# v loaded in rows of four tokens and put in place by TensorE, with score products of a quarter of the keys each

## The chip, the cores and the metric

The kernel runs on one core of one Trainium2 chip. The metric is the device time of one launch in microseconds. A profiled execution gives the span from the first to the last instruction and a trace of every instruction and every DMA packet. The engines are PE (TensorE matmul; PEld its weight loads), DVE (VectorE), ACT (ScalarE), POOL (GpSimd) and SP (SyncE, which issues most DMAs here).

## What is computed

There are 8 batches, 8 heads, 576 tokens and 64 values per head. First a sliding-window attention with a linear bias per head, then a mixing of the 64 lowest frequencies along the sequence by complex 512x512 weights, one pair of matrices for each frequency, and a last product with a ReLU. q, k, v, the weights and the output are float32.

```python
scores = scale * np.matmul(q, k.transpose(0, 1, 3, 2))
rel = pos[:, None] - pos[None, :]
mask = (rel >= 0) & (rel < 128)
scores = np.where(mask, scores + bias[None], -1000000000.0)   # bias = -slope(h) * |rel|
attn = softmax(scores)
x = matmul(attn, v), heads side by side                       # (8, 576, 512)
X = np.fft.rfft(x, axis=1)                                    # first 64 modes
Yr = Xr @ w_r - Xi @ w_i ;  Yi = Xr @ w_i + Xi @ w_r          # per mode
u = x + irfft(Y)
out = u + relu(u @ w_ch)
```

## The kernel before

**Units and slots.** The attention is cut into 32 units. A unit is a pair of heads s and a batch b. The first 8 units are head pair 0 for all batches (group 0); the other 24 go batch by batch through head pairs 1, 2, 3 (group 1). A loop runs one slot per unit, and the instructions are placed by hand: `manual_schedule` keeps every engine's order as the program writes it. Slot n works on several units at once: the scores of unit n, the transposes of q and k of unit n+1, the casts of n+2, the product of the weights with v (av) of unit n-1, and the spectrum of unit n-2.

**What one unit needs.** q and k come by one DMA each (`_load_unit`, L356), 9 tokens in a row of 2304 bytes. POOL casts them to bf16 (L391). `_tr` turns them by 18 transposes each on PE (L414) into a PSUM buffer `tqk`, and `_evac` copies that to SBUF on ACT (L422). `_score` makes the scores in two halves w = 0, 1 into one PSUM tile `sc`, of two banks (L441; the last 64 keys at L449); ACT takes the exponential (L453), DVE multiplies with a mask that holds bias and window (L458, L463). `_av` multiplies with v and a column of ones (L487, L493) and DVE divides (L498 to L504). `_spectrum` (L533) turns x into modes: in group 0 after each unit, 5 matmuls, in group 1 after every third, 15 matmuls.

**The keys' order.** In a block of 128 keys the key's token number is spread over the partitions: partition 64 r + p holds token 2 p + r. The two score matmuls of a block and head therefore read every second key, and the rows of `sc` come out in that order; the mask's distance has a step of -2 per partition, and 127 is added in the upper half. v has the same order, since two tokens in sequence are one row of 512 bytes in DRAM. `_load_v` (L367) issues two DMAs per unit, one per head, and `_cast_v` (L403) moves and casts it on POOL with four instructions into one of three buffers `vb`, from which av reads. The last 64 tokens (`vt`) come on their own.

**The weights.** A ring of 48 KB in each partition takes the weights in the order of use: 64 parts of 0.5 MB for group 0 (rows of the first head pair), then 64 parts of 1.5 MB for group 1. `_load_w` (L652) issues a part as soon as its space in the ring has been used, from inside `_modes`, whose matmuls are L692 (`acc`). The products of group 0 are spread over the slots from number 10 on (arguments w0 and w1 of `_slot`); `_select` (L572 to L579) prepares their operand every few slots, in a PSUM tile that the spectrum also uses. The products of group 1 follow after the last slot, with other work between them (the product with w_ch, L746, and from the modes that are ready already the first of the inverse transforms, `_z_early`, L779 and L783). A last part, `_finish`, ends the inverse transform and writes the output.

**Order on the queues.** All loads but `vt` go through SP's one queue. Before the slots it gets the loads of 16 units and the first weight parts; in each later slot one more unit, the v of the unit three before it, and the weight parts that have become free. There are nine buffers for q and for k (`QK`) and six for v (`VB`).

In a slot PE's order is: score w = 0, transposes of q, transposes of k, weight products w0, score w = 1, spectrum, av, weight products w1:

```python
    if n < N:
        _score(g, n, 0)
    if n + 1 < N:
        _tr(g, n + 1, 0)
        _evac(g, n + 1, 0)
        _tr(g, n + 1, 1)
```

Of the kernel before, what the change touches and what calls it, by code (L numbers as in the profile page):

```python
# [9 lines left out]
FP32 = mybir.dt.float32  # L10
# [32 lines left out]
def kernel(  # L43
# [50 lines left out]
    with tc.manual_schedule(engines={ET.SP, ET.PE, ET.Activation, ET.DVE, ET.Pool}):  # L94
        with ExitStack() as wctx:
# [5 lines left out]
            with ExitStack() as actx:  # L101
# [3 lines left out]
                if JOINT[0] != 2:  # L105
# [8 lines left out]
                g.ps2 = actx.enter_context(  # L114
                    tc.tile_pool(name="ps2", bufs=1, space=bass.MemoryType.PSUM))
                g.ps1 = actx.enter_context(
                    tc.tile_pool(name="ps1", bufs=2, space=bass.MemoryType.PSUM))
                g.pss = actx.enter_context(
                    tc.tile_pool(name="pss", bufs=1, space=bass.MemoryType.PSUM))

# [10 lines left out]
                with tc.tile_pool(name="tmpc", bufs=1, side="right") as tp:  # L131
                    _consts(g, tp)
                    _cast_qk(g, 0)
                    for s in GROUPS[0]:
                        _load_vt(g, s)
                    _cast_qk(g, 1)
                    _cast_v(g, 0)
                    for s in GROUPS[0]:
                        _cast_vt(g, s)
                    _tr(g, 0, 0)  # L140
                    _tr(g, 0, 1)
                    _evac(g, 0, 0)
                    _evac(g, 0, 1)
                    first = dict.fromkeys(u[1] for u in units[:2])
                    rest = [s for s in range(NP) if s not in first]
                    for s in first:
                        _mask(g, tp, s)
                    for n in range(3):
                        _slot(g, n, [], [])
                    for s in rest:  # L150
                        _mask(g, tp, s)
# [85 lines left out]
def _consts(g, tp):  # L237
# [4 lines left out]
    mi = tp.tile([P, 2, NM], I32)  # L242
    nc.gpsimd.iota(mi, [[0, 2], [1, NM]], base=0, channel_multiplier=0)
    reli = tp.tile([P, 256], I32)
    nc.gpsimd.iota(reli, [[1, 256]], base=0, channel_multiplier=-2)
    rel3i = tp.tile([P, 64], I32)
    nc.gpsimd.iota(rel3i, [[1, 64]], base=0, channel_multiplier=-1)
    make_identity(nc, g.ident_b)
# [37 lines left out]
    rel = tp.tile([P, 512], FP32)  # L286
    g.rel = rel
    nc.vector.tensor_copy(rel[:, 0:256], reli)
    nc.vector.tensor_scalar_add(rel[64:128, 0:256], rel[64:128, 0:256], 127.0)
    nc.vector.tensor_copy(rel[:, 448:512], rel3i)  # L290
    nc.vector.tensor_scalar_add(rel[64:128, 448:512], rel[64:128, 448:512], 64.0)
    off = tp.tile([P, 256], FP32)
# [68 lines left out]
def _load_v(g, n):  # L361

    _, s, b = g.units[n]
    u = g.unit.setdefault(n, Ctx())
    u.v = g.vpool.tile([P, 2, 2, 2, g.D], FP32, tag="v", name=f"v{n}")
    for hh in range(2):
        g.nc.sync.dma_start(  # L367
            out=u.v[:, hh].rearrange("p k r d -> p k (r d)"),
            in_=g.v[b, 2 * s + hh, 0:512, :].rearrange("(k p r) d -> p k (r d)", k=2, r=2))


def _load_vt(g, s):
# [22 lines left out]
def _cast_v(g, n):  # L395

    u = g.unit[n]
    u.vb = g.vbs[n % 3]
    o = u.vb[:, :, 0 : g.D].rearrange("p (k i h) d -> p i k h d", k=2, i=2)
    v = u.v.rearrange("p h k r d -> p r k h d")  # L400
    for r in range(2):
        for i in range(2):
            g.nc.gpsimd.tensor_copy(  # L403
                o[64 * r : 64 * r + 64, i], v[64 * i : 64 * i + 64, r])


def _tr(g, n, w):
# [11 lines left out]
def _evac(g, n, w):  # L419
    u = g.unit[n]  # L420
    dst = g.work.tile([P, g.S], BF16, tag=f"qkT{w}", name=f"qkT{w}")
    g.nc.scalar.copy(  # L422
        dst.rearrange("c (p r) -> c p r", r=g.R), u.tp[w].rearrange("c r p -> c p r"))
    u.qk = getattr(u, "qk", []) + [dst]


def _score(g, n, w):


    nc = g.nc  # L430
    u = g.unit[n]
    s = g.units[n][1]
    qT, kT = u.qk
    sc = g.pss.tile([P, 2, 512], FP32, tag="sc", name="sc")
    for i in range(2):
        c = 2 * w + i
        nq = 256 if c < 3 else 192
        for r in range(2):
            for hh in range(2):
                hs = slice(64 * hh, 64 * hh + 64)  # L440
                nc.tensor.matmul(  # L441
                    sc[64 * r : 64 * r + 64, hh, 256 * i : 256 * i + nq],
                    lhsT=kT[hs, c * P + r : c * P + P : 2], rhs=qT[hs, c * P : c * P + nq],
                    start=True, stop=True, tile_position=(64 * hh, 64 * r))
    if w:
        for r in range(2):
            for hh in range(2):
                hs = slice(64 * hh, 64 * hh + 64)
                nc.tensor.matmul(  # L449
                    sc[64 * r : 64 * r + 64, hh, 448:512], lhsT=kT[hs, 512:576],  # L450
                    rhs=qT[hs, 512:576], start=True, stop=True, tile_position=(64 * hh, 64 * r))
    a = g.work.tile([P, 2, 512], BF16, tag=f"att{w}", name=f"att{w}")
    nc.scalar.activation(a, sc, AF.Exp, scale=1.0 / math.sqrt(g.D))  # L453
    u.att = getattr(u, "att", []) + [a]
    if not w:
        a = a.rearrange("p h (i q) -> p h i q", i=2)
        m = g.mask[:, s, :, 0:256].unsqueeze(2).broadcast_to([P, 2, 2, 256])
        nc.vector.tensor_tensor(out=a, in0=a, in1=m, op=ALU.mult)  # L458
# [124 lines left out]
def _slot(g, n, w0, w1):  # L583
# [7 lines left out]
    if n + 1 < N:  # L591
        _tr(g, n + 1, 0)
        _evac(g, n + 1, 0)
        _tr(g, n + 1, 1)
    if n == N + 1:
        _spectrum(g, n - 2)
    for w in w0:
# [1 line left out]
    if n < N:  # L599
        _score(g, n, 1)  # L600
    if n + 1 < N:
        _evac(g, n + 1, 1)
    if n + 2 < N:
        _cast_qk(g, n + 2)
    if n + 1 < N:
        _cast_v(g, n + 1)
    for j, grp in enumerate(GROUPS[1:]):
        for i, s in enumerate(grp):
            if n == g.first[j + 1] - 4 + i:
# [324 lines left out]
```

## Time and profile before

| | |
|---|---|
| median of 3 runs | 455.17 us (453.47 to 456.06) |
| the profiled execution's own time | 454.71 us |
| its span, first to last instruction | 452.9 us |
| mean granted clock of TensorE | 0.787 |
| attention: first exponential, last av | 11.8 us, about 165 us |
| weight products of group 1 | from about 169 to 413 us |
| the end (`_finish`) | 413 to 453 us |
| DMA in all | 173.85 MB, 51273 packets, mean 384 GB/s |
| of it v without its last 64 tokens | 64 DMAs of 128 KB, 16384 packets of 512 bytes |
| POOL in the casts of v (L403) | 128 of 498 ns mean, 63.7 us |

Busy times are shares of one engine's time; several engines are busy at once. In a group of instructions "idle before" is how long the engine stood still ahead of them, and after the arrow what ended it. The DMA share is the sum of the packets' times over 16 engines and the stretch, so it can be somewhat above 1 where packets overlap. The clock is the share of TensorE's full clock that was granted.

### The profile page before, as it was taken

The numbers are of one execution on the slowest core, as the hardware profiler recorded it, in microseconds if no ns is written. First come the engines' busy times: TensorE is split into PE (matmuls) and PEld (weight loads), VectorE is DVE, ScalarE is ACT, GpSimd is POOL, SyncE is SP. The second block draws the span as 40 slices with busy tenths as digits, with TensorE's granted clock in tenths as the row PEclk, the third lists the DMA queues.
The fourth block names the chain that finished last, engine by engine and source line by source line (L and its number), as shares of the span: only waits on it lengthen the run. The fifth ranks groups of instructions, "written<-read, shape, count | busy, mean of one in ns | idle before, by whom it ended". The sixth has DMA issues, their size and how long they took to land.

```text
span 452.9 us, 12955 instructions
## 1 busy us (share of the span) xinstructions
PE 303.4 (67%) x5543; PEld 205.8 (45%) x5543; DVE 221.0 (49%) x434; ACT 191.4 (42%) x302; POOL 151.5 (33%) x262
## 2 busy tenths in 40 slices
PE   2677788887888873225555656657555657777994
PEld 2565576666676762213333333333333334554562
DVE  8467757647575561012433443435434334552784
ACT  4887677656665821001222332223222122332773
POOL 7799789866785502020000000000000000002574
PEclk9988859856797975556888886888667568998999
DMA  8999999999999999999999999999999999991778
GB/s 253 353 348 310 387 314 379 377 388 371 390 364 399 415 416 433 422 432 428 431 426 429 428 430 424 430 429 431 425 430 428 431 425 430 429 419 63 271 266 299
DMA packets 51273, 173.85 MB, mean 384 GB/s; under 512 B 4880, under 2 KB 21264, under 8 KB 43024
## 3 DMA queue, kind: packets, MB, share of 16 engines
q1 hardware_dynamic: 50832, 171.99, 96.1%
q0 software_dynamic: 384, 1.05, 0.9%
q8 instruction: 43, 0.70, 0.6%
q14 instruction: 14, 0.11, 0.1%
HBM read 163.58 MB, written 9.44 MB: 382 GB/s over the span
## 4 chain that ended last, share of the span: by engine, by line
DMA 46%; PE 27%; ACT 11%; DVE 9%; issue 4%; POOL 2%; POOLq 0%; ACTq 0%; DVEq 0%
DMA ring<-in_moe_w_r_dram 37%; DMA ring<-in_moe_w_i_dram 9%; ACT att L453 6%; PE acc L692 4%; PE sc L441 4%; PE xt L533 3%; PE av L487 3%; ACT qkT L422 3%; PE tqk L414 2%; PE mm L830 2%; PE y L830 1%; PE mm L733 1%; PE xw L746 1%; DVE att L463 1%; DVE x_sb L501 1%
## 5 line engine op out<-in xcount | busy, mean ns | idle before, releaser
L692 PE MATMUL acc<-Xz,ring 128*128 128x32 bf16 x2048 | 69.7, 183 | 95.9 <-DMA ring<-in_moe_w_i_dram 48.3
L692 PEld LDWEIGHTS <-ring 128*128 128x128 bf16 x2048 | 60.4, 101 | 126.8 <-DMA ring<-in_moe_w_i_dram 61.5
L751 ACT CAST hl<-xw 64x512 bf16<-64x512 f32 x72 | 41.8, 581 | 125.3 <-PE xw L746 93.2
L752 DVE TENSOR_TENSOR hl<-xw,hl 64x512 bf16<-64x512 f32 x72 | 49.6, 689 | 63.5 <-ACT hl L751 63.1
L453 ACT ACTIVATE att<-sc 128x1024 bf16<-128x1024 f32 x64 | 65.6, 1025 | 31.5 <-PE sc L441 25.2
L403 POOL CAST vb<-v 64x256 bf16<-64x256 f32 x128 | 63.7, 498 | 22.4 <-PE av L487 15.3
L772 POOL MEMSET ZTa<- 32x512 bf16 x1 | 0.5, 515 | 189.4 <-ACT ZTa L769 189.4
L746 PE MATMUL xw<-wch,xT 128*128 128x512 bf16 x144 | 52.4, 502 | 0.2 <-ACT FT L346 0.2
L441 PE MATMUL sc<-qkT,qkT 64*64 64x256 bf16 (+1 forms) x512 | 32.6, 330 | 25.8 <-ACT qkT L422 15.3
L422 ACT COPY qkT<-tqk 128x576 bf16<-128x576 bf16 x64 | 40.7, 637 | 0.6 <-PE tqk L414 0.5
L414 PE MATMUL tqk<-ident_b,qkb 64*64 64x64 bf16 x1152 | 31.8, 215 | 8.4 <-POOL qkb L391 8.3
L414 PEld LDWEIGHTS <-qkb 64*64 64x64 bf16 x1152 | 31.3, 131 | 11.1 <-POOL qkb L391 10.4
L458 DVE TENSOR_TENSOR att<-att,mask 128x1024 bf16<-128x1024 bf16 x32 | 27.5, 858 | 13.2 <-ACT att L453 13.1
L487 PE MATMUL av<-vb,att 128*128 128x65 bf16 (+1 forms) x512 | 31.2, 216 | 1.5 <-DVE att L463 0.8
L579 ACT ACTIVATE Xz<-xz 128x192 bf16<-128x192 f32 (+1 forms) x24 | 7.5, 313 | 54.3 <-DVE Xz L578 54.0
L726 DVE COPY xT<-tp 128x512 bf16<-128x512 bf16 x36 | 15.2, 422 | 30.3 <-PE tp L724 30.0
L391 POOL CAST qkb<-q 128x576 bf16<-128x576 f32 x32 | 26.4, 825 | 5.4 <-PE tqk L414 1.8
L487 PEld LDWEIGHTS <-att 128*128 128x128 bf16 (+1 forms) x512 | 24.6, 112 | 7.0 <-DVE att L463 1.2
L441 PEld LDWEIGHTS <-qkT 64*64 64x64 bf16 x512 | 13.2, 120 | 30.7 <-ACT qkT L422 17.7
L391 POOL CAST qkb<-k 128x576 bf16<-128x576 f32 x32 | 26.1, 817 | 0.1
L463 DVE TENSOR_TENSOR att<-att,mask 128x1024 bf16<-128x1024 bf16 x32 | 25.1, 785 | 1.5 <-ACT att L453 1.1
L746 PEld LDWEIGHTS <-xT 128*128 128x128 bf16 x144 | 17.1, 125 | 18.3 <-issue 14.0
(108 smaller groups left out, 424.0 us busy)
## 6 DMA issues: line engine op xcount, KB each, us to landing
ring<-in_moe_w_r_dram SPq DMA_DIRECT2D x32, 1536.0 KB, 13.8
ring<-in_moe_w_i_dram SPq DMA_DIRECT2D x32, 1536.0 KB, 13.8
ring<-in_moe_w_r_dram SPq DMA_DIRECT2D x32, 512.0 KB, 6.8
ring<-in_moe_w_i_dram SPq DMA_DIRECT2D x32, 512.0 KB, 7.2
q<-in_q_dram SPq DMA_DIRECT2D x32, 288.0 KB, 6.7
k<-in_k_dram SPq DMA_DIRECT2D x32, 288.0 KB, 6.3
v<-in_v_dram SPq DMA_DIRECT2D x64, 128.0 KB, 5.7
out_dram<-o SPq DMA_DIRECT2D x32, 256.0 KB, 2.7
```

What stands on the lines that cost most here:

```text
L391: g.nc.gpsimd.tensor_copy(tb, t)
L403: g.nc.gpsimd.tensor_copy(o[64 * r : 64 * r + 64, i], v[64 * i : 64 * i + 64, r])
L414: g.nc.tensor.transpose(tp[hs, r, :], u.b[w][hs, r], g.ident_b[hs, hs], tile_position=(64 * hh, 64 * hh))
L422: g.nc.scalar.copy(dst.rearrange("c (p r) -> c p r", r=g.R), u.tp[w].rearrange("c r p -> c p r"))
L441: nc.tensor.matmul(sc[64 * r : 64 * r + 64, hh, 256 * i : 256 * i + nq], lhsT=kT[hs, c * P + r : c * P + P : 2], rhs=qT[hs, c * P : c * P ...
L453: nc.scalar.activation(a, sc, AF.Exp, scale=1.0 / math.sqrt(g.D))
L463: g.nc.vector.tensor_tensor(out=a, in0=a, in1=g.mask[:, g.units[n][1]], op=ALU.mult)
L487: nc.tensor.matmul(av[o, hh, col(t)], lhsT=att[c // 2][:, hh, q0 : q0 + m], rhs=u.vb[:, 2 * c + hh, 0 : D + 1], start=(j == 0), stop=(t < ...
L692: nc.tensor.matmul(acc[:, et, :, m0 - c0 : m0 - c0 + n, :], lhsT=wt[:, a, et * P : (et + 1) * P], rhs=X[:, a, 1 - w : 3 - w, m0 % MB : m0 ...
L746: nc.tensor.matmul(xw, lhsT=xT[:, dt], rhs=g.wch[:, dt], start=(dt == 0 and g.way[n] != "q"), stop=(dt == 3))
L751: nc.scalar.copy(g.hl[own, n, h], xw[own])
L752: nc.vector.tensor_tensor(out=g.hl[other, n, h], in0=xw[own], in1=g.hl[own, n, h], op=ALU.subtract)
```

## The change

v comes in rows of four tokens: 1024 bytes, one DMA per unit instead of two. In a block of 128 keys partition 32 r + p now holds token 4 p + r, so a score matmul takes a quarter of a block's keys, and there are twice as many of them, each on 64 rows and 32 columns of the array. The mask's distances follow. A row of v lies in the wrong partitions, so POOL only casts it, in one instruction, to a new tile `vc` (one unit earlier than before), and a new function `_place_v` puts it in place: 16 matmuls whose stationary side is 32 columns of the identity, each into a group of 32 columns, into a PSUM tile `vp`; then one copy to `vb`, on ACT for odd units and on DVE for even ones. To make room in PSUM there is one `tqk` buffer where there were two, and the transposes of k move behind the second score, with `_place_v` after them.

```diff
-                    tc.tile_pool(name="ps1", bufs=2, space=bass.MemoryType.PSUM))
+                    tc.tile_pool(name="ps1", bufs=1, space=bass.MemoryType.PSUM))
...
+                    _cast_v(g, 1)
                     for s in GROUPS[0]:
                         _cast_vt(g, s)
-                    _tr(g, 0, 0)
-                    _tr(g, 0, 1)
-                    _evac(g, 0, 0)
-                    _evac(g, 0, 1)
+                    for w in range(2):
+                        _tr(g, 0, w)
+                        _evac(g, 0, w)
+                    _place_v(g, 0)
...
-    nc.gpsimd.iota(reli, [[1, 256]], base=0, channel_multiplier=-2)
+    nc.gpsimd.iota(reli, [[1, 256]], base=0, channel_multiplier=-4)
...
-    nc.vector.tensor_scalar_add(rel[64:128, 0:256], rel[64:128, 0:256], 127.0)
+    for r in range(1, 4):
+        rs = slice(32 * r, 32 * r + 32)
+        nc.vector.tensor_scalar_add(rel[rs, 0:256], rel[rs, 0:256], 127.0 * r)
...
-    u.v = g.vpool.tile([P, 2, 2, 2, g.D], FP32, tag="v", name=f"v{n}")
-    for hh in range(2):
-        g.nc.sync.dma_start(
-            out=u.v[:, hh].rearrange("p k r d -> p k (r d)"),
-            in_=g.v[b, 2 * s + hh, 0:512, :].rearrange("(k p r) d -> p k (r d)", k=2, r=2))
+    u.v = g.vpool.tile([P, 2, 4, g.D], FP32, tag="v", name=f"v{n}")
+    g.nc.sync.dma_start(
+        out=u.v.rearrange("p h r d -> p h (r d)"),
+        in_=g.v[b, 2 * s : 2 * s + 2, 0:512, :].rearrange("h (p r) d -> p h (r d)", r=4))
...
 def _cast_v(g, n):
     u = g.unit[n]
+    u.vc = g.work.tile([P, 4, 2, g.D], BF16, tag="vc", name="vc")
+    g.nc.gpsimd.tensor_copy(u.vc, u.v.rearrange("p h r d -> p r h d"))
+
+
+def _place_v(g, n):
+    nc = g.nc
+    u = g.unit[n]
     u.vb = g.vbs[n % 3]
-    o = u.vb[:, :, 0 : g.D].rearrange("p (k i h) d -> p i k h d", k=2, i=2)
-    v = u.v.rearrange("p h k r d -> p r k h d")
-    for r in range(2):
-        for i in range(2):
-            g.nc.gpsimd.tensor_copy(
-                o[64 * r : 64 * r + 64, i], v[64 * i : 64 * i + 64, r])
+    ps = g.ps1.tile([P, 4, 2, g.D], FP32, tag="vp", name="vp")
+    for c in range(4):
+        cs = slice(32 * c, 32 * c + 32)
+        for r in range(4):
+            nc.tensor.matmul(
+                ps[32 * r : 32 * r + 32, c].rearrange("p h d -> p (h d)"),
+                lhsT=g.ident_b[:, cs], rhs=u.vc[:, r].rearrange("p h d -> p (h d)"),
+                start=True, stop=True, tile_position=(0, 32 * r))
+    o = u.vb[:, :, 0 : g.D].rearrange("p (c h) d -> p c h d", c=4)
+    if n % 2:
+        nc.scalar.copy(o, ps)
+    else:
+        nc.vector.tensor_copy(o, ps)
...
-        for r in range(2):
+        for r in range(4):
             for hh in range(2):
                 hs = slice(64 * hh, 64 * hh + 64)
                 nc.tensor.matmul(
-                    sc[64 * r : 64 * r + 64, hh, 256 * i : 256 * i + nq],
-                    lhsT=kT[hs, c * P + r : c * P + P : 2], rhs=qT[hs, c * P : c * P + nq],
-                    start=True, stop=True, tile_position=(64 * hh, 64 * r))
+                    sc[32 * r : 32 * r + 32, hh, 256 * i : 256 * i + nq],
+                    lhsT=kT[hs, c * P + r : c * P + P : 4], rhs=qT[hs, c * P : c * P + nq],
+                    start=True, stop=True, tile_position=(64 * hh, 32 * r))
...
         _tr(g, n + 1, 0)
         _evac(g, n + 1, 0)
-        _tr(g, n + 1, 1)
...
     if n < N:
         _score(g, n, 1)
     if n + 1 < N:
+        _tr(g, n + 1, 1)
         _evac(g, n + 1, 1)
+        _place_v(g, n + 1)
     if n + 2 < N:
         _cast_qk(g, n + 2)
-    if n + 1 < N:
-        _cast_v(g, n + 1)
+        _cast_v(g, n + 2)
```

## The prediction

> **What bounds the kernel now.** I read the page first, then busy times by stretch, then SP's waits, then the chain around the end of the attention, and last PE's timeline of single slots.
>
> ```profile
> span 452.9 us, 12955 instructions
> ...
> DMA  8999999999999999999999999999999999991778
> GB/s 253 353 348 310 387 314 379 377 388 371 390 364 399 415 416 433 422 432 428 431 426 429 428 430 424 430 429 431 425 430 428 431 425 430 429 419 63 271 266 299
> ...
> DMA 46%; PE 27%; ACT 11%; DVE 9%; issue 4%; POOL 2%; POOLq 0%; ACTq 0%; DVEq 0%
> ```
>
> The DMA row is at 9 from the second slice to the 36th, about 412 us: the queue never runs dry. Only the rate changes, 310 to 399 GB/s while q, k and v are mixed in, about 430 once only weights flow.
>
> ```profile
> 12.00:57.00 45.00, 33.29 (x748) 25.74 (x747) 30.02 (x64) 34.18 (x46) 39.65 (x66) 0.89 1.05 351
> 57.00:166.00 109.00, 90.47 (x2165) 73.60 (x2165) 69.88 (x150) 71.81 (x101) 75.77 (x129) 0.79 1.03 380
> 166.00:412.00 246.00, 143.14 (x2210) 84.47 (x2210) 86.26 (x153) 55.36 (x106) 5.27 (x21) 0.73 1.00 423
> ```
>
> Columns: stretch, its length, busy PE, PEld, DVE, ACT, POOL, granted clock, DMA share, GB/s. The attention (12 to 165) has a DMA share of 1.03 to 1.05 and engines that are 60 to 90% busy: two things run side by side, a full DMA queue and a compute chain that lives on what was loaded ahead. SP's waits from 60 to 166 tell which is ahead:
>
> ```profile
> SPq L356 <- DMA ring<-in_moe_w_i_dram: 8.7, 10, 0.9
> SPq L652 <- PE acc L692: 5.6, 11, 1.5
> SPq L367 <- DMA q<-in_q_dram: 5.3, 10, 1.7
> ```
>
> SP waits more for earlier landings than for PE to free the ring. The first ring space was free when its products ended at 58.2 us; SP issued into it at 67.08. So compute is ahead of the issue, and DMA sets the pace; the lead is used up only at the end:
>
> ```profile
> 164.90 0.36 PE acc L692 x10
> 165.26 11.07 DMA ring<-in_moe_w_r_dram
> ...
> 177.24 13.74 DMA ring<-in_moe_w_r_dram
> ```
>
> At 165.26 SP issues a 1.5 MB part the moment PE frees its space, and it lands 11.07 us later. Its own transfer takes 3.66 us at 430 GB/s, and the quickest q load (288 KB, 0.69 us of transfer) took 3.1 us to land, so 2.4 us are overhead. The rest, **5.0 us**, it stood behind other transfers. This is the margin: compute may end the attention later by 5.0 us less what DMA gains before DMA runs dry. After 166 everything hangs on the 64 large weight parts in sequence and a tail of 41 us that the change does not touch. With g the DMA time saved and s the slip of the attention's end:
>
> change = -g + max(0, s + g - 5.0).
>
> If s is over 5 - g, it is s - 5, whatever g is.
>
> **The DMA part, g.** By the packet records of the trace, 16384 packets of 512 B took 28.5 ns each, 29.2 us on each of 16 engines; 8192 of 2304 B took 103.0, 8192 of 12288 B 461. After it there are 8192 of 1024 B: on the line between 512 and 2304 that is 49.8 ns, 25.5 us; 32 DMAs fewer save 512 completion packets of 9.5 ns, 0.3 us. g = 29.2 - 25.5 + 0.3 = **4.0 us**. Bounds: 0, if a 1024 B packet costs two of 512; 9.5, if it moves at the 12288 B rate (38.4 ns, 19.7 us). I take 4, the nearest rows. [...]
>
> **POOL.** Four casts of 64x256 (498 ns) become one of 128x512: the rows of 128x512 are 617 and 714 ns. That frees about 1.3 us of POOL per unit. It counts only where PE waits for POOL's q and k casts (slots 6 to 9, of 4.67, 4.25, 5.19 and 5.52 us between the first exponentials of L453). With POOL gone PE or ACT sets them at about 4.3 to 4.6, the last with a selection: **-1.2 us**. The cast also no longer waits for av (15.3 us of POOL idle), and DVE's mask products, 858 and 785 ns against 690 when POOL rests, may shorten: **-0.7**, between 0 and -3.
>
> **PE, the place matmuls.** The nearest row is 16 matmuls of 128x32 by 128, zp:
>
> ```profile
> 392.70 1.03 PE L746 MATMUL xw<-wch,xT 128*128 128x512 bf16 x4
> 393.66 0.47 PE L783 MATMUL zp<-ident_b,ZT 128*32 128x128 bf16 x16
> 393.95 1.05 PE L779 MATMUL zwp<-wch,ZT 128*32 128x512 bf16 x16
> ```
>
> zp holds PE from 393.66 to 393.95, 0.29 us at full clock; at half, by four steps of 0.106 as in zlp at 414.9, 0.43. The step from the last xw (393.35) to zp is 0.31 where xw follow each other by 0.215: a change of tile shape costs 0.095 (0.12 at half clock, from the transposes to acc at 94.2). After the change the order is score 64x32, transposes 64x64, weight products 128x128, score 64x32, last keys and transposes 64x64, place 128x32, av 128x128: three to four such changes more per unit, 0.3 to 0.4 us.
>
> **PE, the scores.** Twice the matmuls, 64x32. Four of 64x64 now start within 10 ns and the next four 0.13 to 0.20 us later, so four column groups side by side cost nothing more; zp's four at once speak for it. If eight don't run at once, it costs up to 0.25 us per score, 16 us in all. I take 0.
>
> **PE, the moved transposes.** With one tqk buffer the k transposes wait for ACT's copy of q and stand behind the second score. Behind them on PE wait place, spectrum, av and the next score. What that costs depends on the slot:
>
> ```profile
> 76.28 0.39 PE L441 MATMUL sc<-qkT,qkT 64*64 64x256 bf16 x8
> 76.47 0.23 PE L449 MATMUL sc<-qkT,qkT 64*64 64x64 bf16 x4
> 76.62 0.78 PE L487 MATMUL av<-vb,att 128*128 128x65 bf16 x16
> 77.33 0.22 PE L493 MATMUL av<-vbt,att 64*64 64x65 bf16 x2
> 78.35 0.41 PE L441 MATMUL sc<-qkT,qkT 64*64 64x256 bf16 x8 [0.80 <-ACT qkT L422]
> ```
>
> Here (full clock, no spectrum) PE is idle 0.80 us before the next score. After: q copied at 76.75, k transposes 76.81 to 77.1, place to 77.5, av to 78.3: the idle time hides all but **0.1 us**. ACT's copy of v (0.59, odd units) falls where ACT waits 0.52 for the score; DVE's (0.69, even units) where DVE waits for av. At half clock with a spectrum nothing hides it:
>
> ```profile
> 112.06 0.32 PE L449 MATMUL sc<-qkT,qkT 64*64 64x64 bf16 x4
> 112.31 0.61 PE L533 MATMUL xt<-F,x_sb 128*128 128x128 bf16 x4
> ```
>
> The first score is bound by ACT there before and after, so the transposes taken from ahead of it give nothing back: 0.24 wait and drain, 0.48 transposes, 0.55 place with its drain, less what overlaps, 1.1 us.
>
> **The sum for s.** From slot 10 on: five spectrum slots that no selection holds up (two mixed at 0.5, three at half clock at 1.0): 4.0. Three without spectrum near half clock at 0.5: 1.5. Fourteen others at 0.1, idle PE covering them (without that cover 0.9 each): 1.4. Slots 1 to 5, where short spectra fill PE: 2.0. Two more 32-row adds (0.29 each) in DVE's chain ahead of the masks: 0.6. ACT's copies past the score and more PE instructions to fetch (issue waits): 0.4. Sum 9.9, less 1.9 for POOL and DVE: **s = 8.0**. Then the change is -4.0 + (8.0 + 4.0 - 5.0) = **+3.0 us**. The profiled execution took 454.71 us (span 452.9), 0.46 under the median of the runs, 455.17; the forecast is 457.7 on its scale and **458.2** on the median's.
>
> **Rivals.** *Hidden compute, faster.* If fewer drains are paid, or POOL's relief is larger, s is 1 or less and all of g is gained: -4.0, 451.2. For: PE is idle 18.5 of 109 us from 57 to 166, which pays 0.84 us per slot. Against: the idle time lies in slots that ACT binds, not in the spectrum slots. It decides at s = 5: under that the change gains. *Nothing hidden, much slower.* Place and drain 0.39, three more drains 0.3, wait for the q copy 0.25, in 28 slots: 26 us; less 1.9 and the 5 of margin, near +19, 474; with half of the slots hidden +8. For: PE is already the busiest engine. [...] *The clock.* From 57 to 166 it is 0.79; were the denser PE granted 1.0, the half-clock slots would lose a microsecond each, s would be under 0 and the time 451. Against: slots 18 and 21 ran at 0.50 with PE over 90% busy. [...]
>
> **Numbers.** Forecast (s from 5.5 to 13, +0.5 to +8) 0.50; hidden 0.26; nothing hidden 0.12; line rate 0.07; clock 0.05. Half a per cent, 2.3 us, is about what a measurement here can tell. Faster by more: 0.26 and 0.05 less 0.03 that end within it, 0.28. Slower by more: 0.12, and 0.40 of the forecast's 0.50. Within: the rest, 0.20. The range reaches from 450.5 (full gain, g nearer 5) to 467 (half of the slots unhidden and a little more); the likeliest case alone is 455.7 to 463.
>
> **What would show it.** v's packets are half as many at about 50 ns. The DMA to landing of the part issued at the attention's end falls from 11.07 toward 6 us, and the issue comes near 173. POOL's casts of v take 20 to 23 us in place of 63.7. Slots with a spectrum are about 1 us longer, full-clock slots without it the same. If the attention ends before 168, or the queue stays full with the end after 173, the sum for s or the margin is wrong; if the score matmuls start four by four, the score term is.

## The result: 32 us slower, and the profile after

| | before | after |
|---|---|---|
| median, 4 runs each | 454.61 us | 486.7 us (484.85 to 489.82) |
| ratio, 95% interval | | 1.0708 (1.066 to 1.0756) |
| span of the profiled execution | 452.9 us | 483.1 us |
| end of the last av | 164.9 us | 195.2 us |
| landing of the last weight part | 412.1 us | 439.4 us |
| from there to the end of the span | 40.8 us | 43.7 us |

Ratios leave out executions that fell in a slower state; medians, here and below, are over all.

The forecast was +3.0 us with a slip s of 8.0 us at the attention's end. The slip is 30.3 us, and 27.3 of it arrive at the last weight part. The stretch behind that part, which the change does not touch, is 2.9 us longer; in the runs e1 to e10 it varies from 39.6 to 42.7. The page of the changed kernel, the rows that answer to those shown of before:

```profile
span 483.1 us, 14948 instructions
...
DMA  8999959989878978999999999999999999992578
GB/s 269 376 337 343 384 195 330 374 313 365 287 248 307 380 275 288 331 417 426 432 427 428 428 427 429 429 427 431 427 431 427 430 428 429 427 425 106 213 275 288
...
q8 instruction: 51, 0.84, 0.7%
...
DMA 45%; PE 36%; ACT 8%; DVE 5%; issue 4%; POOLq 0%; POOL 0%; ACTq 0%; DVEq 0%
```

The DMA row is no longer at 9 throughout: it falls to 5 in the sixth slice and is between 7 and 9 from the ninth to the sixteenth, and the rate falls to 195 and 248 GB/s. PE's part of the chain goes from 27 to 36%. q8 is the queue that carries instructions; its 43 packets of before are 51 now, for 1993 more instructions. Its row of before:

```profile
q8 instruction: 43, 0.70, 0.6%
```

The same stretches of the attention as before, with the same columns:

```profile
12.00:57.00 45.00, 35.29 (x836) 24.14 (x841) 23.82 (x51) 30.72 (x44) 25.07 (x36) 0.95 1.05 360
57.00:166.00 109.00, 95.05 (x2469) 68.76 (x2461) 66.65 (x141) 67.68 (x98) 39.68 (x59) 0.72 0.87 309
166.00:200.00 34.00, 29.17 (x705) 21.65 (x705) 17.73 (x41) 16.52 (x24) 3.11 (x5) 0.75 0.83 305
```

From 57 to 166 us the DMA share falls from 1.03 to 0.87, POOL's busy time nearly by half, and PE's rises by 4.6 us although the slots do less: the attention needs 30 us more. What SP waits for from 20 to 200 us says who is ahead now:

```profile
SPq L670 <- PE acc L710: 74.9, 28, 7.6
SPq L359 <- DMA ring<-in_moe_w_r_dram: 7.7, 6, 2.7
```

Before, from 60 to 166 us, SP waited 5.6 us for PE's `acc`; from 60 to 196 us it is now 71.7 us. The first ring space was free at 70.60 us and SP issued into it at 70.63, where before the issue came 8.9 us late. So DMA overtook compute early in the attention and had to wait for it, and from there each microsecond of PE's is one of the kernel's. PE's waits from 12 to 196 us (engine, line, what ended the wait; microseconds in total, times, the longest):

```profile
PE sc L459 <- ACT att L471: 15.3, 24, 2.8
PE av L505 <- issue: 6.6, 7, 1.9
PE tqk L432 <- issue: 2.6, 2, 1.4
PE sc L459 <- ACT qkT L440: 1.5, 3, 0.6
PE sc L467 <- issue: 0.7, 1, 0.7
PE sc L459 <- issue: 0.5, 1, 0.5
```

"issue" is a wait for nothing that the profile shows. They are 10.7 us in twelve places. Before, from 12 to 165 us, they were 1.1 us in two:

```profile
PE sc L441 <- ACT qkT L422: 13.5, 17, 2.1
PE sc L441 <- ACT att L453: 9.7, 10, 3.0
PE sc L449 <- issue: 0.7, 1, 0.7
PE av L487 <- issue: 0.5, 1, 0.5
```

In the middle of an av it looks like this (start, duration, then the idle time ahead in brackets):

```profile
92.93 0.48 PE L505 MATMUL av<-vb,att 128*128 128x65 bf16 x10
95.29 0.46 PE L505 MATMUL av<-vb,att 128*128 128x65 bf16 x6 [1.88 <-issue]
```

Ten of the sixteen matmuls run, PE stands still for 1.88 us, and the other six follow. They read the same two tiles as the first ten, and the profile shows nothing that they waited for.

**PE's budget.** From 12 us to the end of the last av the time is PE's busy time, its issue waits and its other idle time. The three add up, so the table shows where each kernel's slip comes from. The kernels between before and after, and e9, are described below. The last row counts, of the 32 groups of av, those that took over 1.0 us from the first start to the last end, less the idle time inside them: at half speed it is 1.20 us, at full speed 0.78. Each column is one execution. Those of one kernel differ by some us (485 to 490 for after, 465 to 470 for e2, 457 to 464 for e6), so small differences between columns mean little.

```
                   before  rows  moved  shapes  old sc  scores  no place  64 instr  after  big tr  big tr
                           e1    e4     e6      e3      e8      e2        e5               e10     after e9
PE busy             123.2 123.3  124.1  147.0   131.2   139.2   146.4     151.9     155.4  156.7   162.3
issue waits           1.1   1.1    0.3    0.2     6.1     4.8     3.3      13.3      10.7    0.0     1.9
other idle           28.6  28.7   31.5   17.8    25.7    21.8    20.5      13.4      17.1   13.6    16.3
end of last av      164.9 165.1  167.9  177.0   174.9   177.8   182.2     190.6     195.2  182.2   192.5
half-speed av          14    13     14     25       8      15      22        25        17     29      19
```

The change adds 32.2 us of busy PE and 9.6 us of issue waits, and PE's idle time gives back 11.5. If each matmul is counted from its start to the next one's start, or to its own end where that comes first, the 32.2 us are 15.2 in the place matmuls, 6.5 more in the scores, 5.8 more in the transposes and 4.7 in the rest. The slip grows all along: the av of unit 4 starts 8.3 us later than before, that of unit 13 16.3, that of unit 22 22.6, and the last ends 30.3 later.

### The profile page after: what moved, and what is told of

It reads as the page before. It is cut to its first block, busy times and chain, and to the rows that moved or that the text cites. A ratio compares the mean times of both kernels' runs of the same rounds, so it can differ in the third digit from the quotient of the medians.

```text
span 483.1 us, 14948 instructions
## 1 busy us (share of the span) xinstructions
PE 335.6 (69%) x6546; PEld 219.4 (45%) x6567; DVE 229.6 (48%) x452; ACT 199.3 (41%) x318; POOL 103.3 (21%) x166
## 4 chain that ended last, share of the span: by engine, by line
DMA 45%; PE 36%; ACT 8%; DVE 5%; issue 4%; POOLq 0%; POOL 0%; ACTq 0%; DVEq 0%
DMA ring<-in_moe_w_r_dram 34%; DMA ring<-in_moe_w_i_dram 11%; PE av L505 6%; ACT att L471 6%; PE sc L459 6%; PE acc L710 4%; PE xt L551 4%; PE tqk L432 3%; PE vp L414 3%; PE mm L848 2%; PE mm L751 2%; PE y L848 1%; PE sc L467 1%; PE av L511 1%; PE y L751 1%
## 5 line engine op out<-in xcount | busy, mean ns | idle before, releaser
L769 ACT CAST hl<-xw 64x512 bf16<-64x512 f32 x72 | 41.8, 580 | 124.9 <-PE xw L764 94.6
L764 PE MATMUL xw<-wch,xT 128*128 128x512 bf16 x133 | 50.2, 512 | 3.3 <-issue 2.6
L459 PE MATMUL sc<-qkT,qkT 64*32 64x256 bf16 (+1 forms) x1024 | 33.9, 340 | 17.5 <-ACT att L471 15.3
L432 PE MATMUL tqk<-ident_b,qkb 64*64 64x64 bf16 x1152 | 38.5, 220 | 9.6 <-POOL qkb L393 4.8
L432 PEld LDWEIGHTS <-qkb 64*64 64x64 bf16 x1152 | 32.2, 133 | 20.0 <-issue 13.6
L505 PE MATMUL av<-vb,att 128*128 128x65 bf16 (+1 forms) x512 | 33.2, 222 | 6.9 <-issue 6.6
L393 POOL CAST qkb<-q 128x576 bf16<-128x576 f32 x32 | 24.9, 778 | 52.7 <-issue 41.5
L505 PEld LDWEIGHTS <-att 128*128 128x128 bf16 (+1 forms) x512 | 26.4, 116 | 13.9 <-issue 7.6
L744 DVE COPY xT<-tp 128x512 bf16<-128x512 bf16 x36 | 15.2, 422 | 31.4 <-PE tp L742 31.0
L476 DVE TENSOR_TENSOR att<-att,mask 128x1024 bf16<-128x1024 bf16 x32 | 25.7, 804 | 6.8 <-ACT att L471 6.8
L393 POOL CAST qkb<-k 128x576 bf16<-128x576 f32 x32 | 21.9, 684 | 26.6 <-PE tqk L432 22.0
L516 DVE RECIPROCAL rec<-av 128x8 f32<-128x8 f32 x32 | 6.7, 209 | 41.9 <-PE av L511 41.9
L481 DVE TENSOR_TENSOR att<-att,mask 128x1024 bf16<-128x1024 bf16 x32 | 24.8, 774 | 1.7 <-ACT att L471 1.2
L401 POOL CAST vc<-v 128x512 bf16<-128x512 f32 x32 | 21.2, 663 | 15.8 <-DMA v<-in_v_dram 13.4
```

The source lines that it names most:

```text
L393: g.nc.gpsimd.tensor_copy(tb, t)
L432: g.nc.tensor.transpose(tp[hs, r, :], u.b[w][hs, r], g.ident_b[hs, hs], tile_position=(64 * hh, 64 * hh))
L459: nc.tensor.matmul(sc[32 * r : 32 * r + 32, hh, 256 * i : 256 * i + nq], lhsT=kT[hs, c * P + r : c * P + P : 4], rhs=qT[hs, c * P : c * P ...
L481: g.nc.vector.tensor_tensor(out=a, in0=a, in1=g.mask[:, g.units[n][1]], op=ALU.mult)
L505: nc.tensor.matmul(av[o, hh, col(t)], lhsT=att[c // 2][:, hh, q0 : q0 + m], rhs=u.vb[:, 2 * c + hh, 0 : D + 1], start=(j == 0), stop=(t < ...
L764: nc.tensor.matmul(xw, lhsT=xT[:, dt], rhs=g.wch[:, dt], start=(dt == 0 and g.way[n] != "q"), stop=(dt == 3))
```

## The experiments

### Parts of the change (e1 to e4)

**e1_rows_only**: only the load of v is changed, on before.

```diff
+    u.v = g.vpool.tile([P, 2, 4, g.D], FP32, tag="v", name=f"v{n}")
+    g.nc.sync.dma_start(
+        out=u.v.rearrange("p h r d -> p h (r d)"),
+        in_=g.v[b, 2 * s : 2 * s + 2, 0:512, :].rearrange("h (p r) d -> p h (r d)", r=4))
...
+    v = u.v.rearrange("p h (k r) d -> p r k h d", k=2)
```

> The kernel before, with v in rows of 1024 bytes and one DMA per unit; the four casts keep their shapes and read the rows as they lie, so v is left out of place. PE, ACT and POOL do what they did before. If a 1024-byte packet costs about 50 ns and the DMA queue sets the time, the time falls by 4 us, to about 450.6. If 512 bytes are at line rate already, or if compute ends the attention no earlier than the queue can use, it stays at 454.6.

Measured: 453.01 us, ratio 0.9944 (0.9898 to 0.999), by the ratio 2.5 us less (0.5 to 4.6). Packets of 1024 bytes took 48.2 ns; two of 512 had taken 57.0 (28.5 each). The chain around the attention's end:

```profile
165.06 0.36 PE acc L691 x10
165.42 9.08 DMA ring<-in_moe_w_r_dram
```

The attention ends at 165.1, as before, and the part issued there lands in 9.08 us where it took 11.07. So longer rows do gain time, about 2 to 2.5 us; the forecast of 4.0 lies within the interval, and no gain at all lies just outside it.

**e2_no_place**: after without `_place_v`; POOL casts straight into `vb`, of which there are four.

```diff
+    u.vb = g.vbs[n % 4]
+    g.nc.gpsimd.tensor_copy(
+        u.vb[:, :, 0 : g.D].rearrange("p (c h) d -> p c h d", c=4),
+        u.v.rearrange("p h r d -> p r h d"))
...
-        _place_v(g, n + 1)
```

> The changed kernel without the placing: POOL casts straight to vb (a fourth buffer), no place matmuls and no copy from PSUM; v is left out of place. PE work theory (what stands behind the second score on PE is paid in full): 0.39 to 0.55 us of place and drain for 32 units come back, 12 to 18 us, so 469 to 475. Instruction theory (PE waits for its instructions to be fetched): half of the 64 added instructions per unit go, and half of the 10.7 us of issue waits on top: 465 to 470. Clock theory (PE falls to half speed more often because of the new order): most of the loss stays, over 478.

Measured: 467.16 us, 1.0231 (1.0148 to 1.0314).

**e3_old_scores**: after with the score matmuls of before.

```diff
-        for r in range(4):
+        for r in range(2):
...
-                    lhsT=kT[hs, c * P + r : c * P + P : 4], rhs=qT[hs, c * P : c * P + nq],
-                    start=True, stop=True, tile_position=(64 * hh, 32 * r))
+                    lhsT=kT[hs, c * P + r : c * P + P : 2], rhs=qT[hs, c * P : c * P + nq],
+                    start=True, stop=True, tile_position=(64 * hh, 64 * r))
```

> The changed kernel with the score matmuls of before (64x64, half of the keys each) and the mask distances that go with them; v and the keys are then in different orders. PE work theory: the scores took the same array time, so only two changes of tile shape (0.2 us) per unit come back, 6 us: 480. Instruction theory: half of the added instructions go, and 5 us more: 475. If the score matmuls of 64x32 themselves are what is slow, most of the 32 us come back: below 465.

Measured: 464.74 us, 1.0188 (1.0104 to 1.0273).

**e4_moved_transposes**: before with one `tqk` buffer and the k transposes behind the second score.

```diff
-        _tr(g, n + 1, 1)
...
     if n + 1 < N:
+        _tr(g, n + 1, 1)
         _evac(g, n + 1, 1)
```

> The kernel before with one tqk buffer and the transposes of k behind the second score, nothing else. PE work theory: 0.25 to 0.7 us per unit, attention later by 8 to 16 us, less the margin of 5: 458 to 466. Instruction theory: no instruction is added, so 455 to 457. If the order alone puts PE at half speed more often (clock theory): attention later by 15 us or more and over 465, with more than 17 of 32 av groups at 1.1 us.

Measured: 457.31 us, 1.0068 (1.0024 to 1.0112); the attention ends 3.0 us later, almost all of it as PE's idle time.

What follows: no one part holds the loss. Adding them one by one moves the attention's end by +3.0 (moved transposes), +7.0 (place and rows on top, e3) or +14.3 (scores and rows on top, e2), and all together by +30.3, which is 6 more than these three. By the medians it is +2.6, +7.4, +9.9 and +32.1 us, 12 more. Rows alone move the end by 0.2. Taken away from the changed kernel, the scores give 22.0 us back and place 19.5. The scores, taken as nothing in the forecast, cost at least as much as place.

### What the scores cost (e5, e6, e8)

The eight score matmuls that stand side by side do start within 24 ns of each other, as was assumed, and the next eight 0.11 to 0.20 us after the first. So the time is not lost between their starts. It lies behind the last of them: the last keys start 0.33 us after the first score matmul where before they started 0.19 after it (the shortest distances over all units; where PE ran at half speed 0.51 against 0.38). The last keys are 64x64 again, so it fits a change of tile shape, at 0.13 us with two scores in each unit, 8.3 us in all. Two suspects were to be tried: that there are twice as many instructions, and that their shape differs from their neighbours'.

**e8_scores_alone**: before with the new score matmuls and mask distances.

```diff
+                    lhsT=kT[hs, c * P + r : c * P + P : 4], rhs=qT[hs, c * P : c * P + nq],
+                    start=True, stop=True, tile_position=(64 * hh, 32 * r))
```

> The kernel before with the score matmuls of the change (64x32, a quarter of the keys, with the mask distances that go with them); v stays in the old order, everything else as before. In the slots of the earlier runs that differ by the scores alone they cost 0.2 us per unit. If that is all: attention until 169 to 172, 456 to 459. If they also bring PE to half speed (clock theory): over 20 of 32 av groups slow, attention until 178 or later, over 464. Instruction theory: issue waits of 3 to 5 us, 459 to 462.

Measured: 463.48 us, 1.0197 (1.0147 to 1.0246). The end slips by 12.9 us: 16.0 us more of busy PE (0.5 per unit), of which the scores themselves have 9.5, at about as many half-speed groups as before (15 against 14), 3.7 more of issue waits, 6.8 given back by idle time.

**e5_instructions**: before with 32 more matmuls of one column per unit, ahead of the first score; each streams a single column.

```diff
+    if not w:
+        for i in range(32):
+            r, hh = i // 2 % 2, i % 2
+            hs = slice(64 * hh, 64 * hh + 64)
+            nc.tensor.matmul(
+                sc[64 * r : 64 * r + 64, hh, i : i + 1], lhsT=g.ident_b[hs, 0:64],
+                rhs=g.ident_b[hs, 0:1], start=True, stop=True, tile_position=(64 * hh, 64 * r))
```

> The kernel before with 32 matmuls of one column more per unit, ahead of the first score, where PE waits for ACT; they read the identity and are written over. 64 PE instructions more per unit, as many as the change adds, no new tile shape, nearly no array time. Instruction theory: issue waits in the attention rise from 1.1 us to about 10 and the attention ends at 172 to 180: 460 to 468. Otherwise: 0.1 to 0.4 us per unit at most, attention until 168 to 175, issue waits under 4 us: 455 to 461.

Measured: 478.1 us, 1.0484 (1.0403 to 1.0566): by the ratio 22 us slower, with as many PE instructions as the changed kernel has and none of its other parts.

```profile
PE sc L439 <- issue: 8.6, 8, 2.2
PE tqk L414 <- issue: 3.1, 2, 2.0
PE sc L448 <- issue: 1.3, 1, 1.3
```

The issue waits are there too, 13.3 us of them, and no longer at av: they belong to no certain operation. But they are not the whole loss. PE is busy 28.7 us longer; 17.9 of that are in the writes to `sc`, where the added matmuls stand, so these do hold PE. 25 groups of av instead of 14 ran at half speed. Idle time gave back 15.2 us. How much of the 22 us the waits alone make, this run does not separate from the rest.

**e6_tile_shapes**: before with a single one-column matmul of 64x32 ahead of each score.

```diff
+    nc.tensor.matmul(
+        sc[0:32, 0, 0:1], lhsT=g.ident_b[0:64, 0:32], rhs=g.ident_b[0:64, 0:1],
+        start=True, stop=True, tile_position=(0, 0))
```

> The kernel before with one matmul of one column in the 64x32 shape ahead of each score: three to four changes of tile shape more per unit, as in the change, for four instructions. If a change of shape costs 0.1 us of PE time, 0.3 to 0.4 us per unit, a third of it hidden: attention until 170 to 174, 457 to 461. If shapes or their gaps put PE at half speed more often: over 20 of 32 av groups slow, attention beyond 176, over 463. If they cost nothing here: 455.

Measured: 460.42 us, 1.0136 (1.006 to 1.0213). Next to no issue waits (0.2 us), but 23.8 us more of busy PE, and 25 av groups at half speed against 14. The stretch from 57 to 166 us:

```profile
57.00:166.00 109.00, 99.28 (x2034) 79.69 (x2033) 65.17 (x139) 66.43 (x94) 74.73 (x129) 0.59 0.99 356
```

The granted clock is 0.59 there, 0.79 before. Four instructions per unit did this; how much of it is the changes of shape and how much the clock, this run cannot say. The profile is that of an execution of 464.15 us.

**What an issue wait is.** In the traces of after, e5, e7, e8 and e9, PE's instructions (matmuls, weight loads and two semaphore instructions at the start) were counted up to each issue wait over 0.2 us and set beside the packets of the instruction queue. The twelve of after, from 12 us to the end of the attention:

```
wait ends, us   idle, ns   PE instructions so far   since the last   last packet of q8, us
 20.04            254              450                                17.66- 18.76
 53.76           1446             1730                1280            51.34- 52.42
 89.37           1006             3266                1536            86.99- 88.12
 95.29           1882             3522                 256            93.03- 94.00
112.78           1587             4290                 768           109.84-111.17
119.25            244             4546                 256           116.81-117.85
147.15            542             5826                1280           144.78-145.73
152.52            457             6082                 256           150.10-151.07
161.35            528             6594                 512           159.15-160.09
179.92           1204             7362                 768           177.75-178.71
184.75            672             7618                 256           182.50-183.46
191.22            853             7874                 256           188.90-189.84
```

Every distance in the attention is a multiple of 256, in all five traces. Each wait ends 1.2 to 1.6 us after a packet of 16,384 bytes has arrived on q8. (Behind the attention after has twelve more waits over 0.2 us, of 0.22 us each at `xw`, that keep no such distance.) In the attention of before, after and e5 one packet lands in each block of 256, 0.3 to 5.5 us after PE has started on it. Over the whole execution of before and of after it is one in each block too. By these counts PE's instructions come in blocks of 256, one packet each, only the next block was brought ahead, and PE stands still where it has used one up before the next is there. The two waits of before, 2304 instructions apart, are of this kind too. Where two blocks in a row ended in a wait, their packets came 4.5 to 7.7 us apart, in 12 of the 19 pairs 5.8 to 6.6. PE went through a block in 6.75 us on average in the attention of before, in 6.84 in e4, in 5.99 after and in 5.88 in e5. Before, then, PE used its blocks up a little more slowly than they came in most of those pairs; the change lets it use them as fast, and in twelve places it waits. The packets themselves took 1.00 us each; why some land only 5.5 us into a block was not tried.

### After with a busier PE, and fewer instructions (e7, e9, e10)

**e7_after_warm**: after with one matmul of 128x128 by 512 columns ahead of the second score, to see whether a denser PE is granted the clock.

```diff
+        warm = g.ps1.tile([P, 512], FP32, tag="vp", name="warm")
+        g.nc.tensor.matmul(warm, lhsT=g.ident_b, rhs=g.mask[:, 0, 0], start=True, stop=True)
```

> The changed kernel with one full matmul (128x128 by 512 columns, result not used) per unit ahead of the second score, where PE waits for ACT. It adds 0.21 us of array time at full speed, 0.43 at half. Clock theory: PE, which waits less, is slow in fewer than 12 of 32 av groups (22 in the changed kernel), the attention ends 10 us or more earlier: below 478. PE work theory: nothing gained, 487 to 496. Instruction theory: two instructions more, 486 to 488.

Measured: 488.39 us against 454.71, 1.0727 (1.0654 to 1.0799). Half-speed groups stay at 17, busy PE rises from 155.4 to 163.1 us, issue waits from 10.7 to 19.3, and other idle time falls from 17.1 to 8.1. From 57 to 166 us the granted clock was 0.79 instead of 0.72; nothing is gained.

**e10_before_big_transposes** and **e9_after_big_transposes**: before and after with the transposes of two neighbouring rows in one, 128x128, which takes 48 instructions per unit away.

```diff
-    for r in range(g.R):
+    for r in range(0, g.R - 1, 2):
+        g.nc.tensor.transpose(
+            tp[:, r : r + 2].rearrange("p r t -> p (r t)"),
+            u.b[w][:, r : r + 2].rearrange("p r d -> p (r d)"), g.ident_b)
+    for r in range(g.R - 1, g.R):
```

> The kernel before with the same transposes: 48 PE instructions fewer per unit. DMA sets its time, so 451 to 456 by both theories. If the larger transposes were themselves faster or slower on the array, the slots without waits (3.6 us at best) show it here: between 3.4 and 3.7 us if they are alike.

> The changed kernel with four transposes of 128x128 (two tokens of both heads at once) in place of sixteen of 64x64 for each of q and k: 48 PE instructions fewer per unit, about the same array time, loads unchanged; heads and tokens are then mixed in the scores, that order is left out. Instruction theory: only 16 instructions per unit more than before, issue waits fall from 10.7 us to under 3, the attention ends at 170 to 182: 460 to 472. PE work theory: issue waits or not, what place and shapes cost stays, 483 to 490.

Measured: e10 470.75 us, 1.0385 (1.0341 to 1.043); e9 482.86 us, 1.0613 (1.0536 to 1.0691). With fewer instructions the issue waits go: 0.0 in e10, and 1.9 us in e9 where after has 10.7. But the time does not come back. The larger transposes hold PE longer, for q or k of a unit 0.46 us instead of 0.39 at full clock and 0.73 instead of 0.61 at half. And PE falls to half speed, in e10 in 29 groups of 32:

```profile
57.00:166.00 109.00, 103.20 (x1422) 70.31 (x1419) 61.82 (x126) 64.04 (x88) 70.00 (x124) 0.51 0.97 348
```

PE is busy 103 of 109 us at a clock of 0.51. So a PE that is at half speed nearly throughout ends the attention 17.3 us later, without any wait for instructions. It is not these transposes alone that bring it there, for e9 has them too:

```profile
102.00:166.00 64.00, 57.42 (x1346) 40.59 (x1342) 43.12 (x90) 44.07 (x64) 30.33 (x39) 0.98 0.98 360
```

From 57 to 102 us e9 had a clock of 0.50, and then 0.98 for 64 us with PE 90% busy. Its attention ends only 2.7 us earlier than in after: 8.8 us of issue waits went, and 6.9 of busy PE came in their place.

### Fewer instructions by another layout (g1 to g3)

In these, q and k of two units share a tile, so that one transpose of 64x128 does the work of two: after in g1, before in g2, and in g3 before with rows of four tokens and the new scores, v being put in place by sixteen copies on POOL and DVE.

```diff
+    hs = slice(64 * (n % 2), 64 * (n % 2) + 64)
...
+            out=g.pair[w, n // 2][hs].rearrange("p h r d -> p h (r d)"),
+            in_=src[b, 2 * s : 2 * s + 2].rearrange("h (p r) d -> p h (r d)", r=g.R))
```

> The changed kernel with q and k of two units in one tile (a unit in 64 partitions, both heads side by side), so that one transpose of 64x128 does what two of 64x64 did: 36 PE instructions fewer per unit, the same columns streamed (9 steps of 64 in place of 9 pairs of 64), the same result. Instruction theory (PE can't pass 256 instructions faster than some 6 us): 28 instead of 64 more than before, so issue waits of 2 to 4 us instead of 10.7, attention until 168 to 178 instead of 195: 457 to 469. PE work theory (place, tile shapes and order cost what they cost): no change, 484 to 490.

> The kernel before with the same pairing: 36 PE instructions fewer per unit, nothing else. The DMA queue sets its time, so 452 to 456 by both theories; by the instruction theory the attention's compute runs ahead more and then waits for the weight parts (it can't end much before 162), by the PE work theory it ends at 165 as it did.

> A candidate to beat both: rows of 1024 bytes and 64x32 scores as in the change, pairing as above, two tqk buffers and the old order of transposes, and v put in place by 16 casts of 32 partitions, eight on POOL and eight on DVE, instead of PE. Four PE instructions per unit fewer than before. Instruction theory: compute no later than before, the gain of the longer rows shows: 450 to 454. PE work theory (scores cost 0.2 to 0.3 us per unit by their shapes): 455 to 461. If the 16 small casts hold up POOL or DVE: over 461.

Measured: 532.39 us for g1, 1.1716 (1.163 to 1.1803), 535.28 for g2, 530.72 for g3, 1.1654 (1.1562 to 1.1745). All three lose some 70 to 80 us, and DMA is what slows down. Each unit's q and k go to 64 partitions there, which is the likeliest cause, though it was not tried alone. The rate of g1:

```profile
GB/s 200 232 277 253 254 229 193 207 232 222 233 225 225 241 219 328 409 385 332 420 431 430 427 428 429 428 430 430 430 427 430 428 428 428 427 429 199 196 270 250
```

For fifteen slices it is 193 to 277 GB/s, where before had 253 to 416, and the packets beside them slow down as well: those of 1024 bytes take 82.6 ns in g1 against 48.1 in after. POOL's casts of v waited 131.2 us for their DMA. On instructions these runs say nothing.

## Why the prediction was wrong, by its own steps

**The failed step is the sum for s**, 8.0 us against 30.3. Most of it is the cover: the forecast priced a slot without cover at 0.9 us and let PE's idle time hide all but 0.1 of that in 14 slots. The slip measured is 0.95 us per slot on average, 1.0 of busy PE and 0.3 of issue waits less 0.36 of idle time. That this is close to 0.9 is luck, since the parts are others. The start and slots 1 to 5 were put at 0.6 and 2.0; the av of unit 4 starts 8.3 us late. Three terms in detail:

*"More PE instructions to fetch (issue waits): 0.4"*, together with ACT's copies, measured 9.6 us. The trace of before held what was needed: the page counts 43 packets of q8, the waits name issue, and 256 instructions took 6.75 us. The step charged the instructions that the change adds and not the rate at which they can arrive. e5 has 12.2 us more of such waits with almost empty instructions.

*"The scores. I take 0."* The reason given was right, the matmuls do run side by side; the cost lies behind them. e8 shows +16.0 us of busy PE and a slip of 12.9. The 0.13 us behind each score is near the 0.095 to 0.12 that the forecast had for a change of tile shape; it counted these changes and then left them to the idle time. The bound of 16 us for the scores was the right size by luck.

*"Fourteen others at 0.1, idle PE covering them."* PE's idle time did cover something, 11.5 us in all. But the additions to it were 41.8 (32.2 busy, 9.6 issue), not the 20 or so that place, shape changes and moved transposes were put at. By av, speed differs little: 17 groups ran at half speed against 14. The slot that was taken as the example, at 76.28 us, is slot 14; the same slot after, again at full clock:

```profile
91.66 0.40 PE L459 MATMUL sc<-qkT,qkT 64*32 64x256 bf16 x16 [0.25 <-ACT att L471]
91.99 0.22 PE L467 MATMUL sc<-qkT,qkT 64*64 64x64 bf16 x4
92.19 0.47 PE L432 MATMUL tqk<-ident_b,qkb 64*64 64x64 bf16 x18
92.59 0.41 PE L414 MATMUL vp<-vc,ident_b 128*32 128x128 bf16 x16
92.93 0.48 PE L505 MATMUL av<-vb,att 128*128 128x65 bf16 x10
95.29 0.46 PE L505 MATMUL av<-vb,att 128*128 128x65 bf16 x6 [1.88 <-issue]
95.68 0.22 PE L511 MATMUL av<-vbt,att 64*64 64x65 bf16 x2
95.83 0.43 PE L459 MATMUL sc<-qkT,qkT 64*32 64x256 bf16 x16
```

From this score to the next it was 2.07 us, the 0.80 of idle time included. Now it is 4.17: the idle time did hide nearly all of the added work, as forecast (2.29 is left without the issue wait, 0.22 more), but 1.88 us of waiting for instructions came on top. Elsewhere there was less to hide in: in slot 4 PE is idle for 0.53 us ahead of the score (36.01 us) and then works through a spectrum at half speed.

**What was right.** The price of place, 0.29 to 0.43 and 0.55 with its drain: counted as above, the place matmuls hold PE for 0.34 us at full clock and 0.55 at half, 15.2 us in all. The packets of 1024 bytes, 49.8 ns forecast, 48.1 measured. POOL's casts of v, 20 to 23 us forecast:

```profile
L401 POOL CAST vc<-v 128x512 bf16<-128x512 f32 x32 | 21.2, 663 | 15.8 <-DMA v<-in_v_dram 13.4
```

The prologue, 0.6 forecast, is 1.0 (first exponential at 12.8 against 11.8). The place where the sum was made was right too: DMA ahead at first, then the slip of the attention's end counted almost in full.

**The margin**, 5.0 us, was too large. In the runs without a gain in DMA the last part lands 9.1 (e6), 9.5 (e8), 14.1 (e10) and 23.3 us (e5) later for slips of 12.1, 12.9, 17.3 and 25.7: 2.4 to 3.4 us are absorbed. In after it is 3.0 of 30.3, so the 2 us that the rows gain alone are not seen in it, as the formula has it for a slip past the margin.

**What would show it** went half and half. The part issued at the attention's end lands 6.8 us after its issue, near the forecast 6, but because the queue had run dry long before: it is issued at 195.60, not near 173. The slots without a spectrum were to stay the same and did not. The score matmuls start eight by eight, and the score term was wrong all the same.

**The rivals.** *Nothing hidden* (+19, a chance of 0.12) came nearest; its 26 us in 28 slots stand against 32.2 us of busy PE, of which idle time gave back a third, and it had no term for instructions. *The clock* is refuted: from 57 to 166 us PE is busy 95.1 us instead of 90.5 and the granted clock is 0.72 instead of 0.79; in e10 it is busy 103.2 us at 0.51. Whether a busier PE is granted more or less the runs do not show, since e10 had 0.51 with PE 95% busy and e9 0.98 for 64 us at 90%. e7 was granted more than after and has no time to show for it. *Hidden compute* fails with s far above 5. The 0.07 of *line rate* went to g = 0 with s under 5. s was 30.3, and the 2 to 2.5 us that e1 gained speak against a g of 0, as does its packet of 1024 bytes, 48.2 ns where two of 512 took 57.0.

**What stays open.** Of the 32.2 us of busy PE the places are known, but how much of each is changes of shape and how much half speed is not settled, nor is what brings PE to half speed: e3, with most of the change in it, had 8 such groups, e6, with four more instructions per unit than before, had 25. That the parts lose more together than apart would fit instructions that come in blocks (issue waits of 1.1 us in all at 6.75 us a block, 10.7 at 5.99), but was not shown apart. No run takes the issue waits away and leaves the rest as it is, so their 9.6 us are a part of the budget and not what their absence would gain. e1 is the only kernel faster than before, and its v does not stand in its place; a cheap way to put it there was not found.

## What to carry to other kernels

Before adding small matmuls, count PE's instructions, weight loads included, against time: here the packets for blocks of 256 came 4.5 to 7.7 us apart where PE waited for two in a row, and the kernel that used a block up in 6.75 us, with 1.1 us of issue waits, had little left. Even matmuls of a single column, 32 more per unit, cost 22 us (e5), with 12.2 us more of issue waits and 28.7 more of busy PE. Count changes of tile shape as work, 0.13 us for each score here. Price a new matmul by the budget of PE's busy, issue and idle time over the whole stretch and not by one slot at full clock, and let idle time pay only for what stands in the same slot. Where compute and transfers run side by side with 3 us between them, a few microseconds saved in the transfers are not worth any work on the busiest engine.

## What the runs showed of the hardware that was not expected

- In before and after one packet of 16,384 bytes lands on q8 for every 256 PE instructions, and in the attention PE's issue waits over 0.2 us, up to 1.9 us in after and 2.7 in e8, stand a multiple of 256 apart. Some fall in the middle of a group whose other matmuls, on the same tiles, have run.
- The profile gives a granted clock of 1.00 for slots 1 to 5 of after, where av took 1.20 us instead of 0.78. The first entry of the clock's record in that trace is at 45.9 us (24.4 in before), and from 20 to 45 us, where there is none, the clock is given as 1.00. So 0.95 and 0.89 for the stretch from 12 to 57 us say little, and the time of a known group is the better witness there.
- From 57 to 166 us e10, with PE busy 103 of 109 us, ran at a granted clock of 0.51, the lowest of all; e9, with the same transposes, ran at 0.98 from 102 to 166 us with PE busy 57 of 64.
- A score of sixteen 64x32 matmuls lets what follows start 0.13 us later than one of eight 64x64, at full and at half clock, though at full clock the sixteen start within 0.16 us (e8 and after).
- In g1, where q and k are loaded into 64 partitions each, the whole queue ran at 193 to 277 GB/s for fifteen slices of 40, and the packets of 1024 bytes beside them took 82.6 ns instead of 48.1.
